# Moving the second norm of block 1 two stages ahead in the MLP chains of block 0

## The chip, the cores and the metric

The kernel runs on one core of a Trainium2 chip. The metric is the device time of one execution in microseconds (us). The profile page and the views quoted below come from one execution taken by the hardware profiler.

Engine names in the profile: PE is TensorE (matmuls), PEld its weight loads, DVE is VectorE, ACT is ScalarE, POOL is GpSimd, SP is SyncE, whose queue issues most of the transfers.

## The reference

One transformer block with conditioned layer norms on 2048 tokens of width 448: attention with 16 heads, then an MLP of width 1792.

```python
mod = (_silu(c) @ w_mod).reshape(c.shape[0], 6, 1, -1)
sa, ca, ga, sb, cb, gb = (mod[:, 0], ..., mod[:, 5])
h = _layernorm(x, axis=-1) * (1 + ca) + sa
x = x + ga * _A_ref(h, A_wqkv, A_wo)            # softmax attention
h = _layernorm(x, axis=-1) * (1 + cb) + sb
x = x + gb * _B_ref(h, B_w1, B_b1, B_w2, B_b2)  # layernorm, dense, gelu, dense
```

The MLP normalises its input once more (`_B_ref` begins with `_layernorm`). Between attention and the first MLP matmul a token thus passes two layer norms, with a scale and a shift between them. Both together are what the kernel's stages below compute, and what the title calls the second norm.

## The kernel before

The 2048 tokens are cut into four blocks of 512, and a block into four tiles `t` of 128 tokens. Attention comes first (16 units of one head group and one block each), the MLP after it, block by block. Matmul operands are kept as a pair of rounded high part (`hi`) and rest (`lo`), so that a product takes three matmuls.

**The MLP loop.** A block `b` runs 14 chains `i`, one for each 128 columns of the hidden width; `n` counts chains over all blocks, so `n` is `i` in block 0. In chain `n`, `mlp1` puts 11 matmuls into one PSUM tile `m` (L396), ACT applies the gelu (L1361, tile `full`), and VectorE makes `hi` (L1364) and `lo` (L1365). `mlp2` takes 12 matmuls (L1384 to L1386) and runs two chains behind (`LAG = 2`): after `mlp1(n)` PE does `mlp2(n-2)`. After the last chain of a block PE transposes the next block's normalised tiles: chunks 0 and 1 ahead of `mlp2(11)`, chunks 2 and 3 behind it (L277).

**What else runs in block 0's chains.** The order of the instructions on each engine is the order in which this code is written; no scheduler moves them.

- `w_prep` prepares the MLP weights just in time: one item in even chains, two in odd ones. An item of the first matrix is a copy on ACT (L1150) and a subtraction on VectorE (L1151). An item of the second is a product on VectorE (L1169), a copy on ACT (L1171) and a subtraction on VectorE (L1172), which waits for that copy. The last four items of the first matrix write the tile `slot_c1h`. Chain 9 prepares the first of them, chain 10 the second, chain 11 the third and fourth; chain 12 reads all four.
- What is left of the last attention unit (`tail`): at `n` = 0 a reciprocal and two transfers on the POOL queue, at 4 a product on POOL (L1019), at 5 a rounding on VectorE (L1029) and a subtraction on POOL (L1030), at 9 to 12 the output projection of one tile each: three matmuls on PE, a copy on ACT (L1052), an addition on POOL (L1053).
- The second norm of block 1, through `lnst[b + 1][0](i)`, one stage for each chain.

**The stages of the second norm** (`ln2_stages`, table `plan`), for tile `t` = 0 to 3:

- stages 0 to 3, `stat(0, t)`: BN_STATS and BN_AGGR on VectorE (L200, L201); in stage 3 also the reciprocal root, one small VectorE operation (L205) and one on POOL (L207)
- stages 4 to 7, `mid(t)`: the tile is normalised on VectorE (L217), then scaled and shifted on POOL (L1086, L1087)
- stages 6 to 9, `stat(1, t)`: the statistics of the result; in stage 9 the root
- stages 10 to 13, `addb(t)`: a bias is added to the residual on POOL (L1095)
- stages 11 and 12, `fin(t)`: two tiles each, normalised on VectorE (L217) with a copy of 64 columns (L1092)

The transposes at the end of the block read what `fin` wrote.

Of the kernel before, what the change touches and what calls it, by code (L numbers as in the profile page):

```python
# [44 lines left out]
def tile_adaln_block(ctx: ExitStack, tc: tile.TileContext, x, wqkv, wo, w1, b1, w2, b2, c, w_mod, out):  # L45
# [771 lines left out]
    for b in range(NB):  # L817
# [12 lines left out]
        for n, (tb, kind, g) in enumerate(tasks):  # L830
# [29 lines left out]
            if more:  # L860
                k = n - (6, 4, 4, 4)[b]

                if b == 0 and n in (0, 1, 3, 4):
                    x = 2 * n if n < 2 else 2 * n - 2
# [341 lines left out]
    lnst = [ln2_stages(b) for b in range(NB)]  # L1206
# [146 lines left out]
    def mlp1(b, i):  # L1353
        q, ii = divmod(i, 4)
        w_hi, w_lo = w1t[q]
        fs = slice(ii * 128, (ii + 1) * 128)
        p = ps_mx()
        ts = terms448(*yT[b], lambda k: w_hi(k)[:, fs], lambda k: w_lo(k)[:, fs])
        mm_acc(p, [(w, y) for y, w in ts])
        gf = sbt("full", [128, 512], bufs=3)  # L1360
        act.activation(gf, p, AF.Gelu_apprx_tanh, bias=b1_col[:, i : i + 1])  # L1361
        ghi = sbt("hi", [128, 512], F32R, bufs=3)
        glo = sbt("lo", [128, 512], F32R, bufs=3)
        dve.tensor_copy(ghi, gf)  # L1364
        dve.tensor_tensor(out=glo, in0=gf, in1=f(ghi), op=ALU.subtract)  # L1365
        gs[(b, i)] = (ghi, glo)

    def mlp2(b, m):

        if m == 0 and b < NB - 1:  # L1370
            om[b] = [s2[:, j] for s2 in (ps_s2(), ps_s2()) for j in range(2)]
        elif m == 0:
            for key in ("s1", "s0"):
                ps_close(key)
            for t in range(4):
                ps_open(f"t{t}")
            om[b] = [ps_tile(f"t{t}") for t in range(4)]
        ghi, glo = gs.pop((b, m))
        q, ii = divmod(m, 4)
        w_hi, w_lo = w2t[q][0](ii), w2t[q][1](ii)  # L1380
        for t in range(4):
            ts = slice(t * 128, (t + 1) * 128)
            pp = om[b][t][:, :D]
            pe.matmul(pp, ghi[:, ts], w_hi, start=(m == 0), stop=False)  # L1384
            pe.matmul(pp, ghi[:, ts], w_lo, start=False, stop=False)  # L1385
            pe.matmul(pp, glo[:, ts], w_hi, start=False, stop=(m == NFT - 1))  # L1386
        if m == NFT - 1:
            for t in range(4):
                ot = xn_t()
                dve.tensor_tensor(out=ot[:, :D], in0=om[b][t][:, :D], in1=acc[b][:, t, :], op=ALU.add)  # L1390
                sp.dma_start(ov[b][:, t, :], ot[:, :D])

    seq = [(b, i) for b in range(NB) for i in range(NFT)]
    for n in range(len(seq) + LAG):
        if n < len(seq):
            b, i = seq[n]
            mlp1(b, i)
            for fn in tail.pop(n, ()):
                fn()
            for _ in range(2 if n % 2 else 1):  # L1400
                w_prep.step()
            if b + 1 < NB:
                lnst[b + 1][0](i)
        ahead = n < len(seq) and i == NFT - 1 and b + 1 < NB
        if ahead:
            for k in range(2):
                lnst[b + 1][1](k)
        if n >= LAG:
            mlp2(*seq[n - LAG])
        if ahead:  # L1410
            for k in range(2, NC):
                lnst[b + 1][1](k)
# [37 lines left out]
```

## Time and profile before

| | |
|---|---|
| runs | 1112.14, 1113.06 and 1167.62 us, median 1113.06 |
| profiled execution | 1112.02 us, span 1110.0 us |
| PE busy | 1098.9 us, 99% of the span |
| VectorE busy | 807.2 us, 73% |
| ACT busy | 693.0 us, 62% |
| POOL busy | 213.9 us, 19% |
| first matmul of MLP block 0 | 815.96 us |
| transposes after block 0's chains | from 881.82 us |
| transposes after block 1's chains | from 954.90 us |

The span reaches from the first to the last instruction; the profiled execution took 2.0 us more than its span. The 1167.62 us run is a disturbed one. The places of this case lie between 816 and 888 us, the stretch in which block 0's chains run.

### The profile page before, as it was taken

Reading aid. Unit: us, or ns where it says so; the run is one execution under the profiler, and the core shown is the slowest. Engines: PE = TensorE matmul, PEld = TensorE weight load, DVE = VectorE, ACT = ScalarE, POOL = GpSimd, SP = SyncE. Lnnn points to the kernel's source line nnn. Section 1 sums busy time; section 2 is a strip of 40 time slices with the busy share of each in tenths; the row PEclk is TensorE's granted clock in tenths of the full one; section 3 lists DMA queues with packets and bytes.
Section 4 is the critical chain, followed back from the end, with each engine's and each line's share of the span. In section 5 each row is a group of like instructions: output and inputs, shape, how many; then the busy total and the mean of one; then the engine's idle time right before and its main releaser. Section 6 shows DMA issues by size and latency. Waiting matters only on the chain.

```text
span 1110.0 us, 20703 instructions
## 1 busy us (share of the span) xinstructions
PE 1098.9 (99%) x8319; PEld 665.7 (60%) x8319; DVE 807.2 (73%) x1394; ACT 693.0 (62%) x877; POOL 213.9 (19%) x214
## 2 busy tenths in 40 slices
PE   8999999999999999999999999999999999999998
PEld 6756775444444444444444454545568888888887
DVE  6968788999999999988888867584558844434322
ACT  4565657888888888888888878677752311111210
POOL 1533333110000000000000020217215414023000
PEclk9999999999999999999999999999999999999999
DMA  9563263120231211221211402112222100000000
GB/s 309 204 195 102 88 204 112 51 68 30 79 94 42 81 34 52 73 83 48 88 31 59 130 24 88 58 30 78 72 82 67 32 34 1 2 32 1 34 1 34
DMA packets 49341, 81.19 MB, mean 73 GB/s; under 512 B 12311, under 2 KB 18702, under 8 KB 49234
## 3 DMA queue, kind: packets, MB, share of 16 engines
q1 hardware_dynamic: 48762, 79.14, 22.6%
q8 instruction: 65, 1.06, 0.4%
q10 hardware_dynamic: 148, 0.46, 0.1%
q0 software_dynamic: 336, 0.28, 0.1%
q14 instruction: 30, 0.25, 0.1%
HBM read 55.04 MB, written 26.48 MB: 73 GB/s over the span
## 4 chain that ended last, share of the span: by engine, by line
PE 95%; DVE 2%; ACT 1%; issue 1%; DMA 1%; SPq 0%; POOL 0%; DVEq 0%; ACTq 0%; POOLq 0%
PE s L1305 23%; PE o L1263 23%; PE m L396 16%; PE pa L396 9%; PE m L476 8%; PE s L1385 3%; PE s L1386 3%; PE s L1384 3%; PE s L476 2%; PE t L1385 1%; PE t L1386 1%; PE t L1384 1%; PE o L277 1%; DMA slot_c<-in_w_mod_dram 1%; DVE mxp L481 1%
## 5 line engine op out<-in xcount | busy, mean ns | idle before, releaser
L481 DVE TENSOR_REDUCE mxp<-m 128x1 f32<-128x512 f32 x563 | 364.6, 685 | 75.5 <-PE m L476 57.7
L1305 PE MATMUL s<-slot_b,slot_a 28*128 28x512 f32 (+1 forms) x3072 | 358.1, 424 | 0.3 <-ACT slot_c0h L1318 0.3
L1305 PEld LDWEIGHTS s<-slot_b,slot_a 28*128 28x128 f32 (+1 forms) x3072 | 210.9, 183 | 172.3 <-ACT slot_c L1318 93.9
L476 PE MATMUL m<-kh,qh 28*128 28x512 f32 x615 | 229.3, 468 | 0.6 <-DVE mxp L481 0.3
L1318 ACT ACTIVATE slot_c<-s 128x1024 f32<-128x1024 f32 x170 | 174.7, 1028 | 53.2 <-PE s L1305 52.3
L1263 PE MATMUL o<-slot_c,v 128*32 128x512 f32 x680 | 178.8, 605 | 0.0
L1361 ACT ACTIVATE full<-m,b_col 128x512 f32<-128x512 f32 x56 | 38.5, 688 | 191.9 <-PE m L396 179.7
L1263 PE MATMUL o<-slot_c1h,v 128*32 128x512 f32 x512 | 134.7, 605 | 0.9 <-ACT slot_c1h L1318 0.9
L1263 PE MATMUL o<-slot_c0h,v 128*32 128x512 f32 x512 | 134.7, 605 | 0.0
L1318 ACT ACTIVATE slot_c0h<-s 128x1024 f32<-128x1024 f32 x128 | 131.5, 1028 | 2.4 <-PE m L396 2.4
L1318 ACT ACTIVATE slot_c1h<-s 128x1024 f32<-128x1024 f32 x128 | 130.7, 1021 | 0.0
L686 DVE TENSOR_REDUCE mxp<-s 128x2 f32<-128x1024 f32 x103 | 126.2, 1226 | 5.1
L1364 DVE CAST hi<-full 128x512 fp32r<-128x512 f32 x56 | 25.5, 456 | 134.5 <-ACT full L1361 134.5
L1318 ACT ACTIVATE slot_d<-s 128x1024 f32<-128x1024 f32 x86 | 88.4, 1028 | 26.2 <-PE s L1305 25.5
L476 PEld LDWEIGHTS m<-kh,qh 28*128 28x128 f32 x615 | 92.0, 182 | 16.6 <-DVE mxp L481 13.1
L1019 POOL TENSOR_TENSOR osb<-osb,osb 128x512 f32<-128x512 f32 x16 | 21.0, 1314 | 363.6 <-DMA osb<-drec 220.9
L1263 PE MATMUL o<-slot_d,v 128*32 128x512 f32 x344 | 90.5, 605 | 0.4 <-ACT osb L1227 0.4
L396 PE MATMUL m<-y,slot_a 128*128 128x512 f32 x160 | 60.6, 395 | 0.0
L481 DVE TENSOR_REDUCE mxp<-ma 128x1 f32<-128x512 f32 x61 | 39.5, 681 | 13.3 <-PE m L476 8.9
L650 DVE CUSTOM_DVE_ANT_0 slot_d0i<-m,slot_d0i 128x512 f32<-128x512 f32 x54 | 37.3, 691 | 15.1 <-PE m L476 9.4
L1365 DVE TENSOR_TENSOR lo<-full,hi 128x512 fp32r<-128x512 f32 x56 | 43.8, 782 | 5.9 <-DVE hi L1364 0.9
L1263 PEld LDWEIGHTS o<-slot_c,v 128*32 128x32 f32 x680 | 24.5, 108 | 39.1 <-issue 36.6
(341 smaller groups left out, 1843.9 us busy)
## 6 DMA issues: line engine op xcount, KB each, us to landing
slot_b<-d SPq DMA_DIRECT2D x32, 256.0 KB
slot_a<-d SPq DMA_DIRECT2D x32, 256.0 KB
d<-lo SPq DMA_DIRECT2D x28, 256.0 KB
d<-hi SPq DMA_DIRECT2D x16, 256.0 KB
osb<-drec SPq DMA_DIRECT2D x15, 256.0 KB
out_dram<-xn SPq DMA_DIRECT2D x16, 224.0 KB
raw<-in_B_w_dram SPq DMA_DIRECT2D x14, 224.0 KB
qh<-d SPq DMA_DIRECT2D x12, 256.0 KB
```

The costliest lines, as they stand in the source:

```text
L396: pe.matmul(p, a, b, start=(i == 0), stop=(i == len(terms) - 1))
L476: pe.matmul(m, qh_sb[(g, qt)][js, i * 128 : (i + 1) * 128], k[js, :], start=True, stop=True)
L481: dve.tensor_reduce(out=mxp[(g, qt)][:, i, j, cch : cch + 1], in_=m, op=ALU.max, axis=AX.X)
L686: dve.tensor_reduce(out=mxp[(g, qt)][:, i, j : j + 2, cch], in_=t, op=ALU.max, axis=AX.X)
L1263: pe.matmul(o[32 * j : 32 * j + 32, :], v_sb[kt // 4][:, kt % 4, 4 * g + j, :], p[j // 2][:, j % 2, :], start=(kt == 0), stop=(kt == NKT - 1),
L1305: pe.matmul(s2[:, jj, :], ks[rows_, kp, kc], qs[rows_, qp, :], start=(term == 0), stop=(term == 2))
L1318: act.activation(pt[hf], s2, AF.Exp, scale=SCALE)
L1361: act.activation(gf, p, AF.Gelu_apprx_tanh, bias=b1_col[:, i : i + 1])
L1365: dve.tensor_tensor(out=glo, in0=gf, in1=f(ghi), op=ALU.subtract)
L1384: pe.matmul(pp, ghi[:, ts], w_hi, start=(m == 0), stop=False)
L1385: pe.matmul(pp, ghi[:, ts], w_lo, start=False, stop=False)
L1386: pe.matmul(pp, glo[:, ts], w_hi, start=False, stop=(m == NFT - 1))
```

## The change

For block 0's chains only, the stages of block 1's norm are issued two chains earlier. Chain 0 issues stages 0, 1 and 2, chain 1 stage 3, chain 2 stage 4, and so on to chain 11, which issues stage 13. Chains 12 and 13 issue none. Inside a chain the stages still come last, behind `mlp1`, the tail and `w_prep`. Blocks 1 and 2 issue as before. No instruction is added or removed.

```diff
             for _ in range(2 if n % 2 else 1):
                 w_prep.step()
             if b + 1 < NB:
-                lnst[b + 1][0](i)
+                ahead = 0 if b else 2
+                for x in range(i + ahead if i else 0, i + ahead + 1):
+                    lnst[b + 1][0](x)
```

The order on VectorE around chains 10 to 12. `slot_c1h` is the weight tile that chain 12 reads; `hi` and `lo` belong to one chain's gelu; L217 with L1092 is one tile of `fin`. Before, starting with `hi` of chain 10:

```order
L1364 CAST hi_11495<-full_11493 128x512
L1365 TENSOR_TENSOR lo_11496<-full_11493,hi_11495 128x512
L1151 TENSOR_TENSOR slot_c1h_11457<-raw_11454,slot_c_2683_11456 128x256
L1364 CAST hi_11538<-full_11536 128x512
L1365 TENSOR_TENSOR lo_11539<-full_11536,hi_11538 128x512
L1151 TENSOR_TENSOR slot_c1h_11457<-raw_11460,slot_c_2683_11456 128x256
L1151 TENSOR_TENSOR slot_c1h_11457<-raw_11508,slot_c_2683_11456 128x256
L217 TENSOR_SCALAR xn_11227<-xn_11227,mv_11312,rs_11467 128x448
L1092 COPY xn_11227<-xn_11227 128x64
L217 TENSOR_SCALAR xn_11274<-xn_11274,mv_11312,rs_11467 128x448
L1092 COPY xn_11274<-xn_11274 128x64
L1364 CAST hi_11588<-full_11586 128x512
```

The same place after the change, again starting with `hi` of chain 10:

```order
L1364 CAST hi_11501<-full_11499 128x512
L1365 TENSOR_TENSOR lo_11502<-full_11499,hi_11501 128x512
L1151 TENSOR_TENSOR slot_c1h_11465<-raw_11462,slot_c_2686_11464 128x256
L217 TENSOR_SCALAR xn_11239<-xn_11239,mv_11235,rs_11382 128x448
L1092 COPY xn_11239<-xn_11239 128x64
L217 TENSOR_SCALAR xn_11289<-xn_11289,mv_11235,rs_11382 128x448
L1092 COPY xn_11289<-xn_11289 128x64
L1364 CAST hi_11548<-full_11546 128x512
L1365 TENSOR_TENSOR lo_11549<-full_11546,hi_11548 128x512
L1151 TENSOR_TENSOR slot_c1h_11465<-raw_11468,slot_c_2686_11464 128x256
L1151 TENSOR_TENSOR slot_c1h_11465<-raw_11514,slot_c_2686_11464 128x256
L1364 CAST hi_11594<-full_11592 128x512
```

`fin` of tiles 2 and 3 moved from chain 12 into chain 10, and `fin` of tiles 0 and 1 from chain 11 into chain 9, just above the rows shown. All four now stand ahead of the last three pieces of `slot_c1h` or among them.

The order on POOL behind the last `mid` (L1087). `acc_10` is the residual of block 3 (L1053, output projection), `acc_8` that of block 1 (L1095, `addb`). Before:

```order
L1053 TENSOR_TENSOR acc_10_93<-acc_10_93,full_11447 128x448
L207 TENSOR_TENSOR rs_11467<-ve_11465,cst_82 128x4
L1053 TENSOR_TENSOR acc_10_93<-acc_10_93,full_11503 128x448
L1095 TENSOR_TENSOR acc_8_91<-acc_8_91,row_b2g_3147 128x448
L1053 TENSOR_TENSOR acc_10_93<-acc_10_93,full_11546 128x448
L1095 TENSOR_TENSOR acc_8_91<-acc_8_91,row_b2g_3147 128x448
L1053 TENSOR_TENSOR acc_10_93<-acc_10_93,full_11596 128x448
L1095 TENSOR_TENSOR acc_8_91<-acc_8_91,row_b2g_3147 128x448 x2
```

After:

```order
L207 TENSOR_TENSOR rs_11382<-ve_11380,cst_82 128x4
L1095 TENSOR_TENSOR acc_8_91<-acc_8_91,row_b2g_3147 128x448
L1053 TENSOR_TENSOR acc_10_93<-acc_10_93,full_11455 128x448
L1095 TENSOR_TENSOR acc_8_91<-acc_8_91,row_b2g_3147 128x448
L1053 TENSOR_TENSOR acc_10_93<-acc_10_93,full_11509 128x448
L1095 TENSOR_TENSOR acc_8_91<-acc_8_91,row_b2g_3147 128x448
L1053 TENSOR_TENSOR acc_10_93<-acc_10_93,full_11556 128x448
L1095 TENSOR_TENSOR acc_8_91<-acc_8_91,row_b2g_3147 128x448
L1053 TENSOR_TENSOR acc_10_93<-acc_10_93,full_11602 128x448
```

Two `addb` operations more now stand ahead of the addition of the third projected tile, which belongs to chain 11.

## The prediction

> **What bounds the kernel now.** I read the page first, then a table of stretches, then the timeline of PE, and only then the engine that PE waits for.
>
> ```profile
> span 1110.0 us, 20703 instructions
> PE 1098.9 (99%) x8319; PEld 665.7 (60%) x8319; DVE 807.2 (73%) x1394; ACT 693.0 (62%) x877; POOL 213.9 (19%) x214
> ```
>
> PE is busy 99% of the span, so a reordering can win only what PE loses in pauses. The moved stages run in block 0's chains, so the question is where PE pauses there. The table of stretches gives each engine's busy time; the first row is one undisturbed period of `mlp1` and `mlp2`.
>
> ```profile
> 826.30:831.30 5.00, 5.00 (x24) 4.33 (x24) 4.26 (x10) 1.71 (x3) 0.00 (x0) 1.00 0.58 184
> 820.80:870.00 49.20, 49.20 (x227) 42.29 (x226) 42.43 (x70) 15.39 (x29) 19.02 (x16) 1.00 0.25 71
> 870.00:887.20 17.20, 16.34 (x82) 13.51 (x81) 14.26 (x23) 6.07 (x12) 9.93 (x7) 1.00 0.09 28
> 887.20:959.00 71.80, 71.80 (x340) 62.06 (x339) 32.53 (x67) 11.60 (x19) 16.32 (x14) 1.00 0.04 14
> ```
>
> PE (first number after the length) has no pause from 820.8 to 870 us, loses 0.86 us from 870.0 to 887.2, and none in block 1's chains. VectorE (third) is busy 42.4 of 49.2 us in block 0's chains, against 32.5 of 71.8 in block 1's: without `w_prep` it has room, with it hardly any. The timeline of PE shows chain 12 and the transposes of block 0, then the same two places of block 1, where nothing disturbs them.
>
> ```profile
> 873.11 0.39 PE L396 MATMUL m<-y,slot_c 128*128 128x512 f32 x1
> 874.32 0.50 PE L396 MATMUL m<-y,slot_c1h 128*128 128x512 f32 x1
> 875.62 0.51 PE L396 MATMUL m<-y,slot_c1h 128*128 128x512 f32 x1
> 876.19 0.57 PE L396 MATMUL m<-slot_e,o_hi 128*128 128x448 f32 x2
> 881.82 0.38 PE L277 MATMUL m<-ident,xn 128*128 128x128 f32 x2
> 882.63 0.33 PE L277 MATMUL m<-ident,xn 128*128 128x128 f32 x1 [0.43 <-DVE xn L217]
> 883.28 0.77 PE L277 MATMUL m<-ident,xn 128*128 128x128 f32 x5 [0.32 <-DVE xn L217]
> 883.80 0.45 PE L1384 MATMUL s<-slot_d0i,hi 128*128 128x448 f32 x1
> ...
> 952.33 0.39 PE L396 MATMUL m<-y,slot_c 128*128 128x512 f32 x1
> 954.90 1.03 PE L277 MATMUL m<-ident,xn 128*128 128x128 f32 x8
> 955.69 0.45 PE L1384 MATMUL s<-slot_d0i,hi 128*128 128x448 f32 x1
> ```
>
> Eight transposes take 883.80 - 881.82 = 1.98 us in block 0 and 955.69 - 954.90 = 0.79 in block 1: PE loses **1.19 us** there, waiting for `fin` (L217). The 11 matmuls of a chain take 954.90 - 952.33 = 2.57 us, those of chain 12 in block 0 876.19 - 873.11 = 3.08: PE loses **0.51 us**, and the rows name `slot_c1h`. So 1.70 us is all that this change could win. VectorE at these places:
>
> ```profile
> 869.62 0.42 DVE L1151 TENSOR_TENSOR slot_c1h<-raw,slot_c 128x256 fp32r<-128x256 f32 x1
> 870.98 0.43 DVE L1364 CAST hi<-full 128x512 fp32r<-128x512 f32 x1 [0.95 <-ACT full L1361]
> 871.51 1.46 DVE L1365 TENSOR_TENSOR lo<-full,hi 128x512 fp32r<-128x512 f32 x1
> 872.89 2.67 DVE L1151 TENSOR_TENSOR slot_c1h<-raw,slot_c 128x256 fp32r<-128x256 f32 x2
> 875.48 0.50 DVE L217 TENSOR_SCALAR xn<-xn,mv,rs 128x448 f32<-128x448 f32 x1
> 876.13 0.51 DVE L217 TENSOR_SCALAR xn<-xn,mv,rs 128x448 f32<-128x448 f32 x1
> 881.24 1.33 DVE L217 TENSOR_SCALAR xn<-xn,mv,rs 128x448 f32<-128x448 f32 x1
> ```
>
> The last pieces of `slot_c1h` end at 875.56 (872.89 + 2.67), and PE goes on at 875.62. One tile of `fin` occupies VectorE 876.13 - 875.48 = 0.65 us. Several operations here are far longer than elsewhere. POOL says why:
>
> ```profile
> 871.01 1.41 POOL L1095 TENSOR_TENSOR acc<-acc,row_b2g 128x448 f32<-128x448 f32 x1
> 872.38 1.60 POOL L1053 TENSOR_TENSOR acc<-acc,full 128x448 f32<-128x448 f32 x1
> 873.95 1.33 POOL L1095 TENSOR_TENSOR acc<-acc,row_b2g 128x448 f32<-128x448 f32 x1
> ...
> L1365 DVE TENSOR_TENSOR lo<-full,hi x56: 691/693/1461, 821.3 to 1100.1; 128x512 fp32r<-128x512 f32 x56
> ```
>
> `lo` takes 0.69 us as a rule and 1.46 at worst, and the long one begins under an `addb` that ends at 872.42, 0.55 us ahead of its own end. The two pieces of `slot_c1h` follow in the same way behind POOL's operations that end at 873.98 and 875.28. VectorE and POOL take turns, and **a collision costs VectorE 1.46 - 0.69 = 0.77 us**.
>
> **The change part by part.** *The transposes.* All four `fin` come two chains earlier, ahead of chain 12. The wait of 1.19 us goes; what is late next is `slot_c1h`.
>
> *`fin` ahead of `slot_c1h`.* Before, all four tiles came behind its last piece; now all four come ahead. That is 4 x 0.65 = 2.60 us more work before a piece for which PE already waits. VectorE stands idle once just before, 0.95 us ahead of `hi` of chain 11 (row 870.98), and a late VectorE uses that up: 2.60 - 0.95 = 1.65 us. All other moved work (statistics, `mid`) stood ahead of the last pieces before and still does, so it adds nothing there.
>
> *Collisions.* Before, two `addb` hit VectorE while it worked towards `slot_c1h` (871.01, 873.95), with the projection's addition between them. Now three `addb` stand ahead of that addition. None of them may hit, or the fourth may join: from two collisions fewer, -1.54 us, to two more, +1.54. I take one more, **+0.77**, the value of one `addb` added to that stretch.
>
> *Statistics under POOL.* Eight statistics move into stretches where POOL works. Whether they collide too is shown by the norm of block 0:
>
> ```profile
> 765.38 0.63 DVE L200 BATCH_NORM_STATS2 st<-xn 128x6 f32<-128x448 f32 x1 [3.38 <-POOL xn L1087]
> ...
> 765.31 1.15 POOL L1086 TENSOR_TENSOR xn<-xn,row_cb 128x448 f32<-128x448 f32 x1
> ```
>
> It ran its usual 0.63 us wholly inside a POOL operation, so I take no collision for them. The Trainium skill (SBUF — State Buffer, section "SBUF: two separate sides") draws the line in the same place: one port pair is locked for a whole instruction, against VectorE operations in a two-port mode or with two SBUF inputs. A rule of "any VectorE operation" would add up to 8 x 0.77 = 6.2 us; the trace is with the page, so the sum leaves that out.
>
> *The front and the middle of the block.* The next rows are `lo` of chain 1, one tile's statistics with what follows, the last piece of `slot_c0h`, and, from the chain that ended last, the 11 matmuls of chain 8 that read it; then POOL's last operation for the projection.
>
> ```profile
> 823.83 0.69 DVE L1365 TENSOR_TENSOR lo<-full,hi 128x512 fp32r<-128x512 f32 x1
> 830.42 0.62 DVE L200 BATCH_NORM_STATS2 st<-acc 128x6 f32<-128x448 f32 x1
> 831.17 0.39 DVE L1364 CAST hi<-full 128x512 fp32r<-128x512 f32 x1
> 847.79 1.64 DVE L1151 TENSOR_TENSOR slot_c0h<-raw,slot_a3h 128x512 fp32r<-128x512 f32 x1
> ...
> 851.32 2.58 PE m L396 x11
> ...
> 843.31 1.68 POOL L1030 TENSOR_TENSOR osb<-osb,o_hi 128x512 fp32r<-128x512 f32 x1 [0.36 <-DVE o_hi L1029]
> ```
>
> Chain 0 gets two statistics more, each of which occupies VectorE 831.17 - 830.42 = 0.75 us, so `lo` of chain 1, ready at 824.52 before, comes 1.5 us later. PE reads it in the second half of the period that begins at 826.30 (first row of the stretches), from 826.3 + 2.57 = 828.9 on, so the 1.5 us is hidden. The lag grows in the middle. The last piece of `slot_c0h` ended at 847.79 + 1.64 = 849.43. Ahead of it now stand two more `mid` (some 0.4 us each: the 0.50 of L217 less the overlap with the next) and two more statistics, 2.3 us, with two or three more collisions, so it ends near 854. Chain 8 starts at 851.32 and needs it for its last two of 11 matmuls, at 851.32 + 9/11 x 2.58 = 853.4. I expect a **new pause of 0.5 to 1.5 us in chain 8**. It costs nothing by itself, since PE would only wait longer for `slot_c1h` in chain 12; without that second wait it would cost its full length.
>
> *POOL and the queues.* Two `mid` with two POOL operations each (1.15 us, row 765.31) now come ahead of the projection's L1019 and so of L1030, which ended at 844.99: 4 x 1.15 = 4.6 us later at most. PE first reads its result behind chain 9, at 851.32 + 5.00 + 2.57 = 858.9. No transfer is moved: the only ones near, POOL's two behind the reciprocal, are issued in chain 0 ahead of every stage.
>
> *The sum.* Last piece of `slot_c1h` later by 1.65 + 0.77 = 2.4 us, so chain 12 ends 2.4 us later; the transposes give back 1.19. **+1.2 us** on the profiled execution's 1112.02 gives 1113.2. The undisturbed runs (1112.02, 1112.14, 1113.06) have a mean of 1112.4, so I forecast a median of **1113.6**.
>
> **The rivals.** *Faster.* VectorE catches up before chain 11 because `addb` has left the stretch 871 to 875. The two collisions gone and nothing else gained: 1.65 - 1.54 = +0.1 at `slot_c1h`, less 1.19: 1110.9; with the 0.51 gone as well, 1110.3. For it: the worst collisions sit exactly there. Against it: POOL's `addb` operations do not vanish, and VectorE is already behind by then.
>
> *Slower: the collisions multiply.* `mid` and `addb` all fall into VectorE's fullest stretch. It decides from the third extra collision on, which the `mid` operations must bring, since `addb` has only two. With four: 1.65 + 4 x 0.77 = 4.7, less 1.19: +3.5, 1115.6. With a fifth it would be 1116.3. For it: VectorE has 49.2 - 42.4 = 6.8 us free in that stretch, much of it in pauses too short to give to anyone. Against it: the number of POOL operations ahead of the place grows by two only.
>
> *Slower: PE's clock falls.* The new pause in chain 12 is 0.51 + 2.4 - about 1 = 2 us, longer than any in this stretch. The granted clock is 1.00 in every row of the stretches; were it halved for one period of 5.00 us, 5 us would be added: 1118. Against it speaks the start of the span:
>
> ```profile
> 0.00:20.00 20.00, 16.47 (x83) 10.53 (x84) 11.09 (x28) 10.79 (x21) 3.08 (x13) 1.00 0.94 311
> ```
>
> PE pauses 3.5 us in those 20, and the clock granted is 1.00. The Trainium skill (TensorE: Matmul & The Clock Gate, section "HAM oscillation — how this bites in real kernels") would let the clock fall only after a pause above about 3.4 us; by that, my 2 us would not reach it. No row here shows such a fall.
>
> *No effect.* The order shows that the stages do move, so the change does what it says; but the loss at `slot_c1h` and the gain at the transposes may cancel: 1112.0.
>
> **How the numbers follow.** Forecast, 1112.3 to 1114.6 (one collision more or less, and the spread of the runs): 0.50. Faster, 1110.3 to 1111.5: 0.22. More collisions, 1114.6 to 1116.3: 0.17. Cancelling: 0.07. Clock: 0.04. The range from 1110.3 to 1117.0 leaves out the clock and the thin ends of the others; its upper end is that of the collisions plus most of the 1.0 us by which undisturbed runs differ. 2% of the time is 22 us, about what a measurement of this kernel can tell from no change, and no case reaches it: faster 0.01, same 0.98, slower 0.01.
>
> **What would show it.** The transposes of block 0 take 0.8 us, with no wait for L217 (else the `fin` step is wrong). The last piece of `slot_c1h` ends 2 to 3 us after 875.56, and PE pauses 1.5 to 2.5 us in chain 12 (else the collisions were counted wrong). PE pauses in chain 8. BN_STATS stays at 0.62 us. Blocks 1 to 3 look as before, shifted. What would prove me wrong: a pause at a place not named here, or chain 12 without one.

## The result

The changed kernel takes 1116.43 us, median of 6 runs (1115.76 to 1117.67), against 1112.14 before (median of 5): a ratio of **1.0039**, 95% interval 1.0028 to 1.0049, or 4.29 us. A sixth run of the kernel before, 1167.62 us, was a disturbed one and is left out. The difference is far below 2%, but it is clear of the scatter: the changed kernel is slower. The forecast was 1113.6, some 1.2 us slower, the range 1110.3 to 1117.0.

The profiled execution took 1117.42 us, 5.40 more than that of before. Of these, 0.84 us lie ahead of the first MLP matmul (816.80 against 815.96), where the order of all instructions is the same; the profiled runs of all kernels below have that matmul between 815.5 and 816.8, so I count this part as scatter. For comparisons with before, 0.84 is taken off the times of this profile.

The timeline of PE in the changed kernel, from chain 8's wait to the first chain of block 1 (start, length, operation, and in brackets the idle time before it and what ended it):

```profile
853.88 0.40 PE L396 MATMUL m<-y,slot_a3h 128*128 128x512 f32 x1
855.37 0.50 PE L396 MATMUL m<-y,slot_c0h 128*128 128x512 f32 x1 [1.09 <-DVE slot_c0h L1151]
...
875.26 0.39 PE L396 MATMUL m<-y,slot_c 128*128 128x512 f32 x1
876.20 0.40 PE L396 MATMUL m<-y,slot_c 128*128 128x512 f32 x1
879.10 0.50 PE L396 MATMUL m<-y,slot_c1h 128*128 128x512 f32 x1 [2.51 <-DVE slot_c1h L1151]
880.91 0.95 PE L396 MATMUL m<-slot_e,o_hi 128*128 128x448 f32 x2
882.03 0.57 PE L1384 MATMUL s<-slot_d0h,hi 128*128 128x448 f32 x1
882.40 0.57 PE L1385 MATMUL s<-slot_b1h,hi 128*128 128x448 f32 x1
883.99 0.36 PE L1384 MATMUL s<-slot_d0h,hi 128*128 128x448 f32 x1
884.19 0.37 PE L1385 MATMUL s<-slot_b1h,hi 128*128 128x448 f32 x1
...
887.78 1.03 PE L277 MATMUL m<-ident,xn 128*128 128x128 f32 x8
888.57 0.45 PE L1384 MATMUL s<-slot_d0i,hi 128*128 128x448 f32 x1
...
891.53 0.60 PE L277 MATMUL o<-ident,xn 128*128 128x128 f32 x4
892.56 0.50 PE L396 MATMUL m<-y,slot_b 128*128 128x512 f32 x1 [0.42 <-DVE y L1120]
```

The transposes go through in 888.57 - 887.78 = 0.79 us: the wait for `fin` is gone. In its place stand a wait in chain 8, one of 2.51 us in chain 12, matmuls that are 0.37 us apart (882.03 to 882.40) instead of 0.20 (883.99 to 884.19), and a wait ahead of block 1's first chain. The table of stretches shows what the slow matmuls are (length, busy us of PE, PEld, DVE, ACT, POOL, then the granted clock):

```profile
876.00:879.00 3.00, 0.59 (x3) 0.15 (x1) 2.83 (x8) 0.00 (x0) 0.45 (x1) 1.00 0.26 76
879.50:880.00 0.50, 0.50 (x4) 0.41 (x3) 0.00 (x0) 0.00 (x0) 0.00 (x0) 1.00 0.00 0
880.60:883.60 3.00, 3.00 (x10) 2.59 (x9) 1.63 (x3) 1.22 (x2) 0.67 (x1) 0.50 0.11 39
880.23:883.63 3.40, 3.40 (x11) 2.89 (x10) 1.66 (x3) 1.22 (x2) 0.70 (x1) 0.50 0.18 55
883.60:890.00 6.40, 6.40 (x35) 5.62 (x34) 2.73 (x5) 1.26 (x2) 0.49 (x1) 1.00 0.01 1
```

**PE's clock fell to half** about 1 us after the pause had ended, and stayed there for 3.4 us. VectorE in chains 9 to 12, with `fin` (L217, L1092) ahead of the last pieces of `slot_c1h`:

```profile
869.78 0.51 DVE L217 TENSOR_SCALAR xn<-xn,mv,rs 128x448 f32<-128x448 f32 x1
870.32 1.15 DVE L1092 COPY xn<-xn 128x64 f32<-128x64 f32 x1
871.39 1.39 DVE L217 TENSOR_SCALAR xn<-xn,mv,rs 128x448 f32<-128x448 f32 x1
872.82 0.20 DVE L1092 COPY xn<-xn 128x64 f32<-128x64 f32 x1
872.93 0.42 DVE L1364 CAST hi<-full 128x512 fp32r<-128x512 f32 x1
...
874.06 1.38 DVE L1151 TENSOR_TENSOR slot_c1h<-raw,slot_c 128x256 fp32r<-128x256 f32 x1
875.37 1.34 DVE L217 TENSOR_SCALAR xn<-xn,mv,rs 128x448 f32<-128x448 f32 x1
877.50 0.42 DVE L1364 CAST hi<-full 128x512 fp32r<-128x512 f32 x1
878.02 0.69 DVE L1365 TENSOR_TENSOR lo<-full,hi 128x512 fp32r<-128x512 f32 x1
878.63 0.76 DVE L1151 TENSOR_TENSOR slot_c1h<-raw,slot_c 128x256 fp32r<-128x256 f32 x2
```

The four `fin` take from 869.78 to 872.93 and from 875.37 to 877.50, together 5.28 us where the prediction counted 2.60. POOL's rows name the partners:

```profile
870.26 1.16 POOL L1053 TENSOR_TENSOR acc<-acc,full 128x448 f32<-128x448 f32 x1 [2.48 <-ACT full L1052]
871.38 1.16 POOL L1095 TENSOR_TENSOR acc<-acc,row_b2g 128x448 f32<-128x448 f32 x1
873.68 1.47 POOL L1053 TENSOR_TENSOR acc<-acc,full 128x448 f32<-128x448 f32 x1 [1.15 <-ACT full L1052]
875.12 1.33 POOL L1095 TENSOR_TENSOR acc<-acc,row_b2g 128x448 f32<-128x448 f32 x1
```

Each of the four operations of VectorE above that takes over 1.1 us waits under one of these four. Even the copy of 64 columns, 0.20 us when alone, takes 1.15. The last two pieces of `slot_c1h`, which before took 2.67 us between two of POOL's operations, now take 0.76: the collisions moved from them to `fin`.

**The budget.** An excess is what two neighbouring starts of PE lie apart beyond the undisturbed spacing (0.234 us for 512 columns, 0.205 for 448, 0.109 for a transpose); excesses of 0.12 us and less are left out of the table.

```
                                    before   after
chain 8, slot_c0h                    0.00     1.26
chain 12, slot_c1h                   0.26     2.67
half clock                           0.00     1.38
transposes, fin                      1.13     0.00
first chain of block 1, y            0.00     0.59
sum                                  1.39     5.90
```

The difference of 4.51 us, with the 0.84 of scatter, accounts for 5.35 of the 5.40 us between the two profiles, and it is near the 4.29 us between the medians. Chain 12 of the kernel before loses 0.51 us in all, as the prediction says; half of that lies in spacings too short for the table. A count without any limit: from the first MLP matmul to the first of block 1, PE takes 887.15 - 815.96 = 71.19 us before, 892.56 - 816.80 = 75.76 after, and 885.22 - 815.64 = 69.58 in the one kernel below that has no excess. So 1.61 us were there to win.

### The profile page after: what moved, and what is told of

Read it like the earlier page. It is cut to its first block, busy times and chain, and to the rows that moved or that the text cites. A ratio compares the mean times of both kernels' runs of the same rounds, so it can differ in the third digit from the quotient of the medians.

```text
span 1115.5 us, 20702 instructions
## 1 busy us (share of the span) xinstructions
PE 1101.4 (99%) x8319; PEld 667.9 (60%) x8319; DVE 808.0 (72%) x1394; ACT 692.8 (62%) x877; POOL 213.0 (19%) x214
## 3 DMA queue, kind: packets, MB, share of 16 engines
q8 instruction: 65, 1.06, 0.4%
## 4 chain that ended last, share of the span: by engine, by line
PE 91%; DVE 5%; issue 1%; ACT 1%; DMA 1%; SPq 0%; POOL 0%; DVEq 0%; ACTq 0%; POOLq 0%
PE s L1305 23%; PE o L1263 22%; PE m L396 14%; PE pa L396 9%; PE m L476 8%; PE s L1384 2%; PE s L1385 2%; PE s L1386 2%; PE s L476 2%; PE t L1385 1%; PE t L1386 1%; PE t L1384 1%; DMA slot_c<-in_w_mod_dram 1%; PE o L277 1%; DVE full L1169 1%
## 5 line engine op out<-in xcount | busy, mean ns | idle before, releaser
L1365 DVE TENSOR_TENSOR lo<-full,hi 128x512 fp32r<-128x512 f32 x56 | 44.1, 788 | 5.6 <-DVE hi L1364 0.5
```

## The experiments

Edits are against the changed kernel where the text says so, otherwise against the kernel before. "Last piece" is the end of the last piece of `slot_c1h`, counted from the first MLP matmul of the same profile: 59.60 us before, 62.59 after.

### The pause filled with matmuls

The changed kernel with `mm_acc`'s hook used in chain 12:

```diff
+        filler = None
+        if (b, i) == (0, 12):
+            fp = ps_o()
+            def filler():
+                for _ in range(8):
+                    pe.matmul(fp, ts[0][1], ts[0][0], start=True, stop=True)
-        mm_acc(p, [(w, y) for y, w in ts])
+        mm_acc(p, [(w, y) for y, w in ts], filler)
```

> The changed kernel with eight matmuls of 512 columns (8 x 0.234 = 1.87 us) put on PE in chain 12, just ahead of the matmul that waits for slot_c1h; they write a free PSUM tile that nobody reads. Theory (the pause in chain 12 lets the clock fall, and the fall costs of its own): PE is idle there for only 2.5 - 1.9 = 0.6 us, the granted clock stays at 1.00 behind it, no matmul takes 0.57 us, and the time is about 1.4 us below the changed kernel's 1116.4, near 1115.0. Rival (the slow matmuls have another cause, or cost nothing because VectorE sets the end): slow matmuls stay, or the time stays at 1116.4.

Measured: 1115.13 us, ratio 1.0026 (1.0017 to 1.0035). PE in chain 12 of this kernel, where L1365 is the line of the filling, and the two stretches that follow:

```profile
876.22 2.03 PE L1365 MATMUL o<-y,slot_c 128*128 128x512 f32 x8
878.89 0.51 PE L396 MATMUL m<-y,slot_c1h 128*128 128x512 f32 x1 [0.64 <-DVE slot_c1h L1151]
```

```profile
879.00:883.00 4.00, 4.00 (x19) 3.54 (x20) 1.75 (x4) 1.20 (x2) 1.13 (x1) 1.00 0.21 57
883.00:890.00 7.00, 7.00 (x41) 6.17 (x41) 3.93 (x6) 2.47 (x5) 0.55 (x1) 1.00 0.00 1
```

PE resumes no earlier, since VectorE is as late as without the filling (last piece 879.17 on a first matmul at 816.59, 62.58). But it is idle for 0.64 us instead of 2.51, and the clock stays at 1.00. The ratio falls by 0.0013, some 1.4 us, as the profile's 1.38 says, though the two intervals overlap. None of this kernel's 11 runs has a mean clock under 0.999, where 5 of 6 of the changed kernel have 0.998. The fall is due to the idle time, not to the work behind it. Two kernels further down settle its price within themselves.

### What makes `slot_c1h` late

Three runs of the changed kernel with parts of the norm put back to their old chains:

```diff
 # only fin back (chains 11, 12)
-            plan.setdefault(11 + t // 2, []).append(lambda t=t: fin(t))
+            plan.setdefault((13 if b == 1 else 11) + t // 2, []).append(lambda t=t: fin(t))
 # only addb back (chains 10 to 13)
-            plan.setdefault(10 + t, []).append(lambda t=t: addb(t))
+            plan.setdefault((12 if b == 1 else 10) + t, []).append(lambda t=t: addb(t))
 # both back: both edits
```

> The changed kernel with fin issued in chains 11 and 12 and addb in chains 10 to 13 as before; only the statistics and mid are two chains early. Theory: the pause in chain 8 stays (about 1.3 us), and since VectorE now waits for PE ahead of chain 11's hi, the pause is no longer covered: slot_c1h is as late behind chain 11 as before (pause about 0.5 us), the transposes wait 1.2 us again, and the time is 1.3 us above the kernel before. Rival (that pause is free, as the prediction put it): no difference from before. In either case the clock stays at 1.00.

> The changed kernel with only fin put back to chains 11 and 12. Theory (the four fin ahead of slot_c1h are most of its lateness): the pause in chain 12 falls from 2.5 us to 1 or less, no clock fall, the transposes wait about 1.2 us again; 1 to 2 us above the kernel before. Rival (the addb collisions are the lateness): pause of 2 us or more in chain 12 and 3 us or more above the kernel before.

> The changed kernel with only addb put back to chains 10 to 13. Theory (fin is most of it, a collision or two the rest): the pause in chain 12 is still 1.5 to 2.5 us, transposes without a wait, 2.5 to 4 us above the kernel before. Rival (addb collisions are the lateness): pause of 1 us or less in chain 12, 1 us or less above the kernel before.

And one of the kernel before with `fin` alone moved, all four tiles into chain 10:

```diff
-            plan.setdefault(11 + t // 2, []).append(lambda t=t: fin(t))
+            plan.setdefault(10 if b == 1 else 11 + t // 2, []).append(lambda t=t: fin(t))
```

> The kernel before with all four fin of block 1 issued at the end of chain 10, ahead of slot_c1h's last two pieces, and nothing else moved. Theory: those pieces come 2.6 - 0.95 = 1.65 us later, the pause in chain 12 grows from 0.5 to about 2.2 us, the transposes lose their wait, no pause in chain 8; 0.5 to 1.5 us above the kernel before, more by up to 1.4 if the clock falls. Rival (fin is harmless, the rest of the change did it): pause in chain 12 under 1 us and 0.5 us or more below the kernel before.

Measured (excess in us from each profile; median against the before of the same call):

```
                      last piece  chain 8  chain 12  clock  transposes  block 1  median     ratio (95%)
before                   59.60      0        0.26     0        1.13       0
after                    62.59     1.26      2.67     1.38     0          0.59    +4.29   1.0039 (1.0028-1.0049)
both back                60.15     1.26      0        0        1.15       0       +0.83   1.0006 (0.9997-1.0016)
only fin back            60.22     1.22      0.30     0        0          0.44    +0.81   1.0003 (0.9994-1.0012)
only addb back           61.58     1.24      1.63     0        0          0.58    +2.24   1.0019 (1.0010-1.0028)
fin alone moved          61.89      0        3.28     1.48     0          0.58    +4.29   1.0038 (1.0024-1.0052)
```

`fin` is the cause: without it the last piece is 0.6 us late, with it alone 2.3, and no more than that is needed for the whole loss. The rival that `addb`'s collisions are the lateness falls.

Three of these runs missed in their time; *only fin back* is taken up below. *Fin alone moved* was to cost 2.9 us at most, fall of the clock included, and cost 4.29: four of `fin`'s operations collided, so that the four tiles took 5.99 us (870.05 to 876.04) and not 2.60. *Only addb back* was to cost 2.5 to 4 us and cost 2.24; its pause of 1.47 us is just under the 1.5 expected, and its clock did not fall.

`addb` by itself moves the last piece by 0.07 us (60.22 against 60.15), but by 1.01 where `fin` is moved too (62.59 against 61.58). Its price is paid in chain 9 both times: there it makes the product of a weight item (L1169) wait, so that it takes 1.56 us instead of 0.61 without `fin`, and 1.57 instead of 0.61 with it. The product in *both back*, then in *only fin back*, and POOL in *only fin back*:

```profile
865.40 0.61 DVE L1169 TENSOR_TENSOR full<-raw,row_gb 128x448 f32<-128x448 f32 x1
```

```profile
865.55 1.56 DVE L1169 TENSOR_TENSOR full<-raw,row_gb 128x448 f32<-128x448 f32 x1
865.05 1.59 POOL L1095 TENSOR_TENSOR acc<-acc,row_b2g 128x448 f32<-128x448 f32 x1
```

In *only fin back* VectorE then no longer waits ahead of chain 11's `hi`, where it waits 0.84 us in *both back* (next rows): the free time takes the price up. With `fin` moved there is no free time left there, and all of it reaches the last piece.

*Both back* answers another question, whether the pause in chain 8 is free. Chain 8 and VectorE ahead of chain 11 in that run:

```profile
854.08 0.50 PE L396 MATMUL m<-y,slot_c0h 128*128 128x512 f32 x1 [1.09 <-DVE slot_c0h L1151]
```

```profile
871.85 0.43 DVE L1364 CAST hi<-full 128x512 fp32r<-128x512 f32 x1 [0.84 <-ACT full L1361]
872.99 2.67 DVE L1151 TENSOR_TENSOR slot_c1h<-raw,slot_c 128x256 fp32r<-128x256 f32 x2
```

Here VectorE waits 0.84 us for chain 11's gelu, which the pause in chain 8 has made later. Half a microsecond of the pause is taken out of chain 12's old wait, which is gone, and the rest is lost: PE takes 887.51 - 815.51 = 72.00 us from the first MLP matmul to block 1 against 71.19 before, 0.81 more; the median is 0.83 above, with an interval that just includes zero. Neither bet was right: free would be 0, uncovered 1.3. In the changed kernel VectorE does not wait there (row 877.50 has no bracket), so there the pause is covered.

*Only fin back* missed in two points. Its time is 0.81 us above before where 1 to 2 were expected, and its interval includes zero. And the transposes did not wait again: the two `fin` of chain 12 no longer collided, and PE was late enough by then.

### One stage ahead

```diff
-                ahead = 0 if b else 2
+                ahead = 0 if b else 1
```

> The changed kernel with one stage ahead instead of two. Theory: two fin come ahead of slot_c1h's last two pieces (1.3 - 0.95 = about 0.4 us later), two behind; the lag in chain 8 is about half (no pause, or under 0.3 us); the transposes have no wait: between 0.8 us below and 0.5 us above the kernel before. Rival (anything ahead costs in proportion): 2 us above the kernel before.

Measured: 1115.01 us, +3.17, ratio 1.0028 (1.0016 to 1.0039). A miss, and neither side's: not break-even, yet the pause in chain 8 is gone. Last piece 61.11, chain 12's excess 2.52, transposes none, block 1 0.58. VectorE and then PE in chain 12:

```profile
872.00 1.37 DVE L1151 TENSOR_TENSOR slot_c1h<-raw,slot_c 128x256 fp32r<-128x256 f32 x1
873.29 1.33 DVE L217 TENSOR_SCALAR xn<-xn,mv,rs 128x448 f32<-128x448 f32 x1
```

```profile
877.03 0.50 PE L396 MATMUL m<-y,slot_c1h 128*128 128x512 f32 x1 [2.35 <-DVE slot_c1h L1151]
```

Again both collide, so the expected 0.4 us became 1.5. The profiled execution kept its clock at 1.00 after a pause of 2.35 us, but not all executions did. Of the seven runs, two have a mean clock of 1.000 and take 1113.7 us (1113.70, 1113.72); five have 0.998 and take 1115.35 on average. The same program with and without the fall differs by **1.6 us**.

### `fin` behind the last piece

The kernel before with `fin` at the end of chain 11, behind all that chain 12 reads, and `addb` in chain 13:

```diff
-            plan.setdefault(11 + t // 2, []).append(lambda t=t: fin(t))
-            plan.setdefault(10 + t, []).append(lambda t=t: addb(t))
+            plan.setdefault(11 if b == 1 else 11 + t // 2, []).append(lambda t=t: fin(t))
+            plan.setdefault(13 if b == 1 else 10 + t, []).append(lambda t=t: addb(t))
```

> The kernel before with all four fin of block 1 at the end of chain 11, behind slot_c1h's last piece, and its four addb in chain 13, behind everything that VectorE owes PE. Theory: slot_c1h is up to 0.5 us earlier, the transposes have no wait (1.2 us less), but the first chain of block 1 then waits about 0.6 us for its normalised tiles, as in the changed kernel: 0.6 to 1.1 us below the kernel before. Rival (nothing can be won here): same time as before within 0.3 us.

And the same with chain 13's weight item issued behind the transposes:

```diff
-            for _ in range(2 if n % 2 else 1):
+            for _ in range((2 if n % 2 else 1) if n != 13 else 0):
                 w_prep.step()
...
             for k in range(2, NC):
                 lnst[b + 1][1](k)
+            if n == 13:
+                w_prep.step()
```

> As the run with fin at the end of chain 11, and the last weight item, whose copy on ACT stands ahead of the copies of the normalised tiles, issued behind the last transposes instead of in chain 13. Theory (that copy, which waits for VectorE, is what the first chain of block 1 waits for): that wait of 0.6 us goes too, and the time is 1.2 to 1.7 us below the kernel before. Rival (the wait has another cause): same as the run without this step.

Measured: 1112.40 us, ratio 1.0005 (0.9996 to 1.0014), and **1110.59 us, ratio 0.9985 (0.9977 to 0.9994)**. The first is a miss: it wins the transposes and loses as much again ahead of block 1, where the excess is 1.86 us and not 0.6. The four `addb`, put out of the way in chain 13, met that chain's `hi` and `lo` there. POOL and VectorE in the first kernel:

```profile
879.27 5.43 POOL L1095 TENSOR_TENSOR acc<-acc,row_b2g 128x448 f32<-128x448 f32 x4
...
883.79 1.46 DVE L1365 TENSOR_TENSOR lo<-full,hi 128x512 fp32r<-128x512 f32 x1
885.17 0.61 DVE L1169 TENSOR_TENSOR full<-raw,row_gb 128x448 f32<-128x448 f32 x1
```

The weight item's product (L1169) waits behind them, and its copy on ACT behind that. ACT in the first kernel, then in the second:

```profile
885.82 0.56 ACT L1171 CAST slot_e<-full 128x448 fp32r<-128x448 f32 x1 [3.10 <-DVE full L1169]
886.29 1.55 ACT L1118 CAST y<-m 128x512 fp32r<-128x512 f32 x3
```

```profile
881.81 1.07 ACT L1118 CAST y<-m 128x512 fp32r<-128x512 f32 x2
...
887.77 0.57 ACT L1171 CAST slot_e<-full 128x448 fp32r<-128x448 f32 x1 [1.78 <-DVE full L1169]
```

In the first, the copies of the transposed tiles (L1118) queue behind the weight item's copy (L1171), which waits for VectorE. In the second they run 3.7 us earlier (counted from the first MLP matmul, 816.44 and 815.64), as soon as PE has made them. PE in the first kernel waits 1.69 us for block 1's tiles; in the second no excess above 0.12 us is left in block 0. PE in the first, then the stretch in the second:

```profile
887.82 0.50 PE L396 MATMUL m<-y,slot_b 128*128 128x512 f32 x1 [1.69 <-DVE y L1120]
```

```profile
870.00:887.20 17.20, 17.20 (x89) 14.98 (x88) 13.75 (x23) 6.26 (x12) 9.32 (x7) 1.00 0.10 27
```

This is the one version that beats both kernels. It wins 1.25 us over before by the medians (0.7 to 2.6 by the interval of the ratio), of the 1.61 that were there to win.

### The weight item in the changed kernel

The last two runs make the same edit of `w_prep` in the changed kernel, once alone and once with the filling.

> The changed kernel with block 0's last weight item issued behind the last transposes instead of in chain 13. Theory (the copy of that item on ACT is what the first chain of block 1 waits for): the pause of 0.6 us ahead of that chain is gone from the trace, everything before it stays (1.3 us in chain 8, 2.5 in chain 12, the clock fall behind it), 0.6 us below the changed kernel, near 1115.8 and 3.4 to 3.9 above the kernel before. Rival (the transposes themselves, or something else, are late): the pause stays.

> The changed kernel with both repairs: eight filling matmuls in chain 12 and the last weight item behind the transposes. Theory (the two losses are separate from each other and from VectorE's lateness): clock at 1.00 throughout, no pause ahead of block 1, left over are 1.3 us in chain 8 and 2.7 in chain 12 (0.8 of it idle, the rest filled) less the 1.6 us that the kernel before lost: 2.3 us above the kernel before, near 1114.3. Rival (the losses overlap): 1115.1, as with the filling alone.

Measured: 1115.33 us, ratio 1.0024 (1.0014 to 1.0034), and 1114.30 us, ratio 1.0019 (1.0010 to 1.0028). In both traces the excess ahead of block 1 is gone. The first is 3.00 us above before where 3.4 to 3.9 was expected, because it again has both kinds of run: four with a mean clock of 1.000, average 1114.22, five with 0.998, average 1115.70, 1.5 us apart. In the second no run has less than 0.999. It is 1.97 us above before, where 2.3 was expected: what remains is VectorE's lateness alone. The two losses are separate: by the medians, the filling alone takes 1.06 of the changed kernel's 4.29 us, the weight item alone 1.29, and both together 2.32, though part of the 1.29 is that the clock fell in fewer runs.

## Why the prediction was right, and where it was wrong

The time lies in the range, in part by luck: the likeliest case was not the one that came. The pause in chain 12, the one in chain 8 and the fall of the clock were all named. The wait ahead of block 1 was not, and by the prediction's own sign (a pause at a place not named) it was wrong there.

- **What bounds the kernel, and what can be won.** Right. Before, PE has no excess in block 0 outside the two places, and a version that removes both wins 1.25 us by the medians and 1.61 in the trace, where 1.70 was the most forecast.
- **The transposes.** Right: 0.79 us, no wait for L217. But "what is late next" was read too narrowly. Behind the transposes stood the weight item's copy on ACT, which had been hidden under the old wait; it took 0.59 us of the 1.19 back.
- **`fin` ahead of `slot_c1h`, and the sum.** This is the step that failed: "chain 12 ends 2.4 us later". It ended 880.91 - 876.19 - 0.84 = 3.9 us later. Its terms were mis-sized. The last piece came 2.99 us later. Most of that is `fin`, 2.29 when it is moved alone: each of its eight operations can collide, and three did, where the sum had charged 0.65 us a tile and put the collisions elsewhere. The rest is close to the 0.62 that the other moved work costs without `fin`, which the sum put at nothing. Then PE waited for the third piece, not the last: behind it PE had six matmuls to do (six times 0.234 us, 1.40), behind the last only two (0.47), which adds most of a microsecond. And 0.2 us of it is already the slower clock.
- **Collisions.** The rule (VectorE and POOL take turns, for a whole operation) held, and the price nearly: 0.83 to 0.96 us in the four long rows of VectorE above, against 0.77. Their number did not follow from counting `addb`. They strike nearly whatever VectorE is doing while POOL is busy, and a late VectorE is always doing something. The runs agree with the Trainium skill's page (SBUF — State Buffer, section "SBUF: two separate sides") that the lock lasts for a whole instruction: a copy of 0.20 us waits like an operation of 0.69. BN_STATS kept its 0.6 us, as forecast (0.61 at 843.71, wholly inside a POOL operation).
- **The pause in chain 8.** Forecast at 0.5 to 1.5 us, measured 1.26, and covered by chain 12's wait in the changed kernel, since VectorE nowhere waits for a gelu between the two. Without that cover it cost 0.8, not "its full length", since half a microsecond of it fell into an older wait.
- **The clock.** The rival "PE's clock falls" came true, at a chance of 0.04, with a price of 1.4 to 1.6 us instead of 5: the half clock lasted 3.4 us, in which a little over half as much was done (matmuls 0.37 us apart instead of 0.20). The argument against it was the mistake. The 3.5 us of pauses in the first 20 us are 1.37 us ahead of the first matmul and many short ones, none above 0.91, so that row said nothing of a pause of 2 us. The rule taken from the Trainium skill (TensorE: Matmul & The Clock Gate, section "HAM oscillation — how this bites in real kernels") put the limit at about 3.4 us of pause; here 2.51 us were enough.
- **"More collisions", 1115.6 to 1116.3** is nearest by its number, but for another reason: about 1.4 us of the loss is clock, which the range left out, and 0.6 the wait ahead of block 1. Without these two the kernel takes 1114.30 us (both repairs), in the forecast's own case. The faster case ends at 1110.4 by its terms, not 1110.3, and 2% is far from the finest step that can be told here: the intervals above reach about 0.1% to each side.

## What to carry to other kernels

Work that is moved earlier on a saturated engine is not moved to a free place: find the next piece that the critical engine waits for, and count every moved instruction that now stands ahead of it, at the length it has while POOL is busy (here up to 1.15 us for a copy of 0.20). When a wait is removed, look for the next one on every engine in the chain (here ACT's queue, hidden under the old wait). Place the moved work directly behind the critical piece rather than ahead of it; here that won only once ACT's queue was cleared too. A pause of PE of some 2.4 us or more can cost beyond its length, since the clock may fall with it; matmuls that nobody reads kept it up here.

## What the hardware showed that was not expected

PE's granted clock fell to 0.50 for 3.4 us with a pause of about 2.4 to 2.5 us, in some runs of a kernel and not in others: in 5 of 6 of the changed kernel, 5 of 7 of the one a stage ahead, 5 of 9 of the one with the weight item moved (by a mean clock of 0.998 against 1.000; the pauses are those of each kernel's one profile, 2.51, 2.35 and 2.51 us). With the longest pause, 3.12 us in the kernel with `fin` alone moved, it fell in all 4. That row of PE is:

```profile
877.65 0.50 PE L396 MATMUL m<-y,slot_c1h 128*128 128x512 f32 x1 [3.12 <-DVE slot_c1h L1151]
```

After pauses of 1.47 us (only `addb` back) and 1.69 us (`fin` at the end of chain 11) the traces show no fall, and no run of these two kernels has a mean clock under 0.999. The point of the fall is not tied to the pause: 1.1 us behind its end in the changed kernel (880.23), 1.5 behind with `fin` alone moved (879.19), and 0.5 ahead of its end in the kernel with the weight item moved (877.99). The Trainium skill (TensorE: Matmul & The Clock Gate, section "What's actually happening") describes an observation window that runs freely, of about 3.4 us, and a fall after an idle one. The free-running window fits the mixture of runs, the wandering point of the fall and its length of 3.4 us; that it must be idle throughout does not fit, since PE was busy for at least 0.9 us of any 3.4 us around the shorter pauses. Where the limit lies between 1.7 and 2.35 us is open: no kernel here pauses for a time between these.
